# Attention scores over row halves in one stretch, and float32r passes for half of block 0

## The chip, the cores and the metric

The kernel runs on one core of a Trainium2 chip. The metric is the device time of one execution in microseconds; three executions of the kernel before gave 608.41, 609.69 and 610.22 us, a median of 609.69. The engines are PE (TensorE; PEld is its weight load), DVE (VectorE), ACT (ScalarE), POOL (GpSimd) and SP, whose queue issues the loads and stores.

## The reference

Attention with a window of 128 keys and 4 sink keys (2 batches, 8 heads, 768 positions, head size 64) feeds a network of 512 to 2048 to 512 with a leaky maximum, and that feeds a router with 8 experts.

```python
keep = is_sink | ((rel >= 0) & (rel < window))
a = softmax(where(keep, q @ k.T / sqrt(64), -1e9))       # per head
x = (a @ v)                                              # 1536 tokens x 512
h = x @ w_in; x = maximum(0.01 * h, h) @ w_out           # w_in 512x2048, w_out 2048x512
e = argmax(x @ w_gate)                                   # 8 experts, 384 places each
out = gate * (relu(x[place] @ w1[e]) @ w2[e])            # w1 512x1024, w2 1024x512
```

Results are held to float32 precision. The weights of the first network and of the experts come as float64.

## The kernel before, in words

The 1536 tokens are 12 tiles of 128 (six per batch), taken in 6 blocks of two tiles. For each block j, `build` walks the 16 column tiles f of the hidden layer: `first` makes 128 hidden columns for the block's 256 tokens in PSUM, `leak` applies the leaky maximum, `split_g` splits the result into a high and a low float32r part, and `second`, two column tiles later, multiplies with w_out and adds into two PSUM banks. A float32 product is kept exact in three float32r passes (high x high, high x low, low x high); block 0 instead takes one float32 pass, since its weights have only just come in.

Block 0 also turns the weights from float64 to float32 on DVE (`convert`, three DVE instructions for each half of a column tile), as they land from HBM. `split` makes the high (ACT) and low (POOL in block 0, DVE later) parts that the later blocks use.

Attention is cut into steps. One or two are put between `first` and `second` of a column tile, so that attention of tiles 2j+2 and 2j+3 runs inside block j. Tiles 0 and 1 ("plain") are done before block 0. A unit is four heads g of one tile t; it is worked off in two pairs pr, two steps apart. `pipeline` gives each function its step:

- `high_k`, `low_k`, `high_q`, `low_q`: high and low parts of k and q side by side, on ACT and DVE or POOL;
- `trans_k`, `trans_q`: eight float32r transposes (twelve for tiles 2 and 3) put both parts of a head on 128 partitions, so that a score is two full-height matmuls: (high, low) and (low, high) of q against (high, low) of k;
- `scores` (L501): four matmuls for a pair, into two of the four PSUM buffers of the tag "att"; ACT copies one half (L506), DVE copies the other under a mask (L513), and takes the maximum (L514);
- `exps` (L219), `norm` (L226, L227 on DVE, then POOL), `trans` (transposes of p, then L543: DVE multiplies by the masks of this tile and the one before; for tiles 2 and 3 ACT copies and POOL masks);
- `pv` (L572): float32 products with v, whose two heads of a pair go to the lower and upper 64 output partitions, that is to two column halves of the array.

The order on PE, ACT, POOL and SP is that of the program; on DVE a scheduler chooses it when the kernel is built. The four PSUM buffers "att" serve all of attention's steps and the router's transposes. In block 0 `first` has one PSUM buffer, later two.

Of the kernel before, what the change touches and what calls it, by code (L numbers as in the profile page):

```python
# [29 lines left out]
HQ = 3  # L30
SINK = 2
# [9 lines left out]
CLEAR_AT, CLEAR = 8, 2  # L41
ROUTE = (2, 5, 9, 10, 11, 14)
# [351 lines left out]
class RingAttention(Attention):  # L394
# [16 lines left out]
    def setup(self):  # L411
# [6 lines left out]
        self.kT = [c.tile([P, self.G, 2, self.W], F32R, name=f"kT{g}") for g in range(self.NG)]  # L418
# [45 lines left out]
        if SC:  # L464
            self.psk = [c.tile([P, 4, 32], F32, name=f"psk{n}") for n in range(2)]
            for t in self.psk:
                nc.gpsimd.memset(t, 0.0)
# [19 lines left out]
    def scores(self, t, g, pr):  # L487
        nc = self.nc
        b, i = divmod(t, self.NT)
        W = self.W  # L490
        pm = self.p["pp"].tile([P, 2, W], F32, tag="pm", name="pm")
        mx = self.p["sm"].tile([P, 2], F32, tag="mx", name="mx")
# [28 lines left out]
    def split_p(self, t, g, pr):  # L521

        pm, _, w = self.pu[t, g, pr]
        st = None
        if t % self.NT and self.SC:
            st = self.psk[pr % 2]
            self.nc.gpsimd.tensor_copy(st[:, 0:2, 0:self.SC], pm[:, :, P:])
        self.pu[t, g, pr] = (pm, st)

    def trans(self, t, g, pr):  # L530
        nc = self.nc
        i = t % self.NT
        pm, st = self.pu[t, g, pr]
        ps = self.p["ps"].tile([P, 3, P], F32, tag="att", name="pps")
        for e in range(2):
            nc.tensor.transpose(ps[:, e, :], pm[:, e, 0:P], self.ident)
        if st is not None:
            nc.tensor.transpose(ps[:, 2, :], st.rearrange("p a s -> p (a s)"), self.ident)  # L538
        n = 2 if i else 1
        pt = self.p["c"].tile([P, 2, 2, P], F32, tag="c", name="pt")[:, 0:n]  # L540
        src = ps[:, 0:2, :]
        if i and t >= EARLY:
            nc.vector.tensor_tensor(out=pt, in0=src.unsqueeze(1).to_broadcast([P, n, 2, P]),  # L543
# [1341 lines left out]
```

## Time and profile before

| | us |
|---|---|
| median of three executions | 609.69 |
| profiled execution, whole | 612.13 |
| its span in the trace | 610.3 |
| PE busy | 578.6 (95%) |
| PEld busy | 499.4 (82%) |
| DVE busy | 383.4 (63%) |
| ACT busy | 310.1 (51%) |
| POOL busy | 179.5 (29%) |

The span is what the trace covers; 1.8 us lie around it. Blocks 0 to 5 fill the span up to about 425 us, the router's end and the experts the rest. A matmul's recorded duration contains its way through the array and overlaps that of the next, so the cost of one in a full row of them is the distance from start to start. A float32 matmul stands in the trace as two records. "128*64" behind an instruction gives the rows and columns of the array that it uses.

### The profile page before, as it was taken

The page shows a single profiled execution, that of the slowest core. Times are in us where ns is not written, and L with a number is a line of the kernel's source. Part 1 is how long each engine was busy: PE and PEld are TensorE (multiplying, and loading weights), DVE is VectorE, ACT ScalarE, POOL GpSimd, SP SyncE. Part 2 cuts the span into 40 slices and gives each one's busy share as a digit, 9 for nine tenths or more (in the row PEclk, how much of TensorE's full clock was granted, in tenths as well). Part 3 has the DMA queues.
Part 4 walks back from the last instruction along what each step waited for, and adds up shares of the span by engine and source line. Part 5 has one row for each costly group of instructions (what it writes and reads, how often), then busy time and mean ns, then how long its engine had stood idle before and what let it go on. Part 6 is the DMA issues. An engine that isn't in the chain of part 4 may idle for free. (4 is left out here: it accounts for less than half of the span.)

```text
span 610.3 us, 11622 instructions
## 1 busy us (share of the span) xinstructions
PE 578.6 (95%) x3889; PEld 499.4 (82%) x3889; DVE 383.4 (63%) x908; ACT 310.1 (51%) x900; POOL 179.5 (29%) x328
## 2 busy tenths in 40 slices
PE   7688888999999999999999999999989999999994
PEld 7575656679989989999999988998788989998783
DVE  4798998368854565556655552276476766655992
ACT  4665555566655455545555433254253634434771
POOL 4425545542343234332432233123110120101110
PEclk9899999899999999999999999999989999999998
DMA  8769989521464402230223025755166766543950
GB/s 235 198 208 247 294 224 295 150 88 52 178 208 134 122 18 70 88 104 20 57 53 109 1 58 169 249 188 164 62 207 201 236 195 202 183 138 110 310 186 13
DMA packets 83564, 91.88 MB, mean 151 GB/s; under 512 B 42964, under 2 KB 51156, under 8 KB 83473
## 3 DMA queue, kind: packets, MB, share of 16 engines
q1 hardware_dynamic: 81488, 85.68, 46.9%
q0 software_dynamic: 1984, 5.13, 2.3%
q8 instruction: 39, 0.64, 0.4%
q14 instruction: 53, 0.43, 0.2%
HBM read 72.01 MB, written 20.09 MB: 151 GB/s over the span
## 5 line engine op out<-in xcount | busy, mean ns | idle before, releaser
L894 PE MATMUL y<-wh,gp 128*128 128x512 f32 x320 | 114.2, 397 | 0.5 <-ACT gp L874 0.5
L876 POOL TENSOR_TENSOR gp<-g,gp 128x256 fp32r<-128x256 f32 x77 | 56.9, 738 | 193.1 <-ACT gp L874 148.6
L848 PE MATMUL hps<-xth,wh 128*128 128x256 f32 x320 | 92.8, 290 | 0.0
L848 PE MATMUL hps<-xtl,wh 128*128 128x256 f32 x320 | 90.2, 282 | 0.0
L848 PE MATMUL hps<-xth,wl 128*128 128x256 f32 x320 | 90.1, 281 | 0.0
L1177 DVE TENSOR_TENSOR cw<-craw,cw 128x512 fp32r<-128x512 f32 x128 | 83.4, 695 | 9.0 <-ACT cw L1175 7.7
L1175 ACT CAST cw<-craw 128x512 fp32r<-128x512 f32 x112 | 63.4, 621 | 23.7 <-PE py L1362 23.0
L894 PEld LDWEIGHTS y<-wh,gp 128*128 128x128 f32 x320 | 60.2, 188 | 11.4 <-ACT gp L874 1.0
L1362 PE MATMUL py<-cw,ht 128*128 128x512 f32 x264 | 63.9, 398 | 0.2 <-DVE ht L1350 0.2
L848 PEld LDWEIGHTS hps<-xth,wh 128*128 128x128 f32 x320 | 60.4, 189 | 3.2 <-issue 0.6
L848 PEld LDWEIGHTS hps<-xtl,wh 128*128 128x128 f32 x320 | 60.3, 189 | 3.1 <-issue 0.7
L894 PE MATMUL y<-wl,gp 128*128 128x512 f32 x160 | 62.7, 392 | 0.0
L864 ACT ACTIVATE g<-hps 128x256 f32<-128x256 f32 x80 | 30.5, 381 | 61.5 <-PE hps L848 60.9
L1313 PE MATMUL ph<-xt,cw 128*128 128x256 f32 (+2 forms) x444 | 59.7, 296 | 1.3 <-DVE xt L1301 1.1
L848 PEld LDWEIGHTS hps<-xth,wl 128*128 128x128 f32 x320 | 60.7, 190 | 0.0
L1313 PEld LDWEIGHTS ph<-xt,cw 128*128 128x128 f32 x444 | 58.2, 195 | 1.8 <-DVE xt L1301 1.3
L1362 PEld LDWEIGHTS py<-cw,ht 128*128 128x128 f32 x264 | 49.1, 189 | 11.5 <-DVE ht L1350 0.7
L865 DVE TENSOR_TENSOR g<-hps,g 128x256 f32<-128x256 f32 x80 | 33.4, 417 | 25.0 <-ACT g L864 24.8
L874 ACT CAST gp<-g 128x256 fp32r<-128x256 f32 x80 | 33.3, 416 | 30.9 <-DVE g L865 30.6
L219 ACT ACTIVATE pm<-pm,mx 128x132 f32<-128x132 f32 (+1 forms) x80 | 31.7, 398 | 32.0 <-DVE mx L514 31.9
L1371 POOL DMA_INDIRECT out<-ys,gt x11 | 11.4, 1033 | 112.6 <-DVE ys L1370 112.6
L543 DVE TENSOR_TENSOR pt<-pps,both 128x512 f32<-128x512 f32 x28 | 19.2, 688 | 31.7 <-PE pps L538 31.7
(211 smaller groups left out, 1118.4 us busy)
## 6 DMA issues: line engine op xcount, KB each, us to landing
craw<-in_moe_w SPq DMA_DIRECT2D x128, 256.0 KB, 3.7
rawi<-in_moe_w_in SPq DMA_DIRECT2D x16, 512.0 KB, 4.4
rawo<-in_moe_w_out SPq DMA_DIRECT2D x16, 512.0 KB, 4.8
places<-zero SPq DMA_DIRECT2D x24, 257.0 KB, 6.7
wh<-wscr SPq DMA_DIRECT2D x16, 256.0 KB, 2.8
wl<-wscr SPq DMA_DIRECT2D x16, 256.0 KB, 3.1
xg<-places SPq DMA_DIRECT2D x12, 257.0 KB, 3.4
natv<-in_v SPq DMA_DIRECT2D x12, 256.0 KB, 6.5
```

The costliest lines, as they stand in the source:

```text
L219: nc.scalar.activation(pm[:, e, 0:w], pm[:, e, 0:w], AF.Exp, bias=mx[:, e:e + 1], accum_out=su[:, e:e + 1])
L543: nc.vector.tensor_tensor(out=pt, in0=src.unsqueeze(1).to_broadcast([P, n, 2, P]), in1=self.both.unsqueeze(2).to_broadcast([P, n, 2, P]), ...
L848: nc.tensor.matmul(ps, lhsT=w, rhs=x, start=(n == 0), stop=(n == len(mm) - 1))
L864: nc.scalar.activation(g, ps, AF.Copy, scale=0.01)
L865: nc.vector.tensor_tensor(out=g, in0=ps, in1=g, op=ALU.max)
L874: nc.scalar.copy(gp[:, 0], g)
L876: eng.tensor_tensor(out=gp[:, 1], in0=g, in1=gp[:, 0].bitcast(F32), op=ALU.subtract)
L894: nc.tensor.matmul(y, lhsT=l, rhs=r, start=(start and n == 0), stop=(stop and n == len(mm) - 1))
L1175: nc.scalar.copy(h, t)
L1177: eng.tensor_tensor(out=l, in0=t, in1=h.bitcast(F32), op=ALU.subtract)
L1313: nc.tensor.matmul(self.ph[f][:, sl], lhsT=self.w[e, "a", h, k][w][:, f * P:(f + 1) * P], rhs=self.xt[:, a, k, sl], start=(m == 0), stop=( ...
L1362: nc.tensor.matmul(self.py[n], lhsT=x, rhs=w, start=(h == 0 and f == 0 and m == 0), stop=(h == self.NH - 1 and f == self.HF - 1 and m == 2))
```

## The change

Four things change.

1. A unit is worked off as a whole, four steps to the next (`GROUP`). `turn` takes the place of the six functions that prepared q and k: two float32 transposes of q and two of k, each with two heads of 64 on 128 partitions, then the high part on ACT and the low part on DVE, straight from PSUM. The low part of k has a tile of its own; `keep_k` also serves tiles 0 and 1.
2. `scores` takes a head in three passes (high x high, high x low, low x high) over the 64 partitions where it lies. The two heads of a pair alternate, into different PSUM buffers, and the unit's twelve matmuls follow one another. They take all four "att" buffers. The reduction and the normalisation act on four heads at once, the latter three steps behind.
3. `trans` masks p on DVE for every tile, with one instruction for each of the two tiles of keys.
4. In block 0, column tiles 8 to 15 are handled in three float32r passes as in later blocks (`in_parts`). Their weights are split two column tiles ahead, by ACT and POOL; `split_x0` splits block 0's tokens once. `leak` of these tiles has its maximum on DVE.

```diff
+GROUP, NORM_AT, TRANS_AT, PV_AT = 4, 3, 5, 7
...
+    def keep_k(self, t, g, ps):
+
+        nc, SC, i = self.nc, self.SC, t % self.NT
+        hi, lo = ([k[:, :, i % 2, 0:P]] + [k[:, :, r, P:] for r in range(2 if i == 0 and SC else 0)]
+                  for k in self.kT[g])
+        for n, (h, l) in enumerate(zip(hi, lo)):
+            if n == 2:
+                nc.gpsimd.tensor_copy(h, hi[1].bitcast(F32))
+                nc.gpsimd.tensor_copy(l, lo[1].bitcast(F32))
+            elif n or t >= self.plain - 1:
+                src = ps[:, :, 0:SC] if n else ps
+                nc.scalar.copy(h, src)
+                nc.vector.tensor_tensor(out=l, in0=src, in1=h.bitcast(F32), op=ALU.subtract)
+
+    def turn(self, t, g):
+
+        nc, NP = self.nc, self.G // 2
+        ps = self.p["ps"].tile([P, 2, NP, P], F32, tag="att", name="qps")
+        for a, nm in enumerate("qk"):
+            for pr in range(NP):
+                x = self.heads(t, g, nm)[:, 2 * pr:2 * pr + 2, :]
+                nc.tensor.transpose(ps[:, a, pr, :], x.rearrange("p a d -> p (a d)"), self.ident)
+        qT = self.p["c"].tile([P, 2, NP, P], F32R, tag="c", name="qT")
+        nc.scalar.activation(qT[:, 0], ps[:, 0], AF.Copy, scale=self.scale)
+        nc.vector.scalar_tensor_tensor(out=qT[:, 1], in0=ps[:, 0], scalar=self.scale, in1=qT[:, 0].bitcast(F32),
+                                       op0=ALU.mult, op1=ALU.subtract)
+        self.qT[t, g] = qT
+        self.keep_k(t, g, ps[:, 1])
...
+    def scores(self, t, g):
+        nc, NP = self.nc, self.G // 2
+        i, W = t % self.NT, self.W
+        pm = self.p["pp"].tile([P, NP, 2, W], F32, tag="pm", name="pm")
+        mx = self.p["sm"].tile([P, NP, 2], F32, tag="mx", name="mx")
         own = i % 2
         w = W if i else P
-        sps = [self.p["ps"].tile([P, 2, W], F32, tag="att", name="sps") for e in range(2)]
-        for e in range(2):
-            h = 2 * pr + e
-            rhs = self.kT[g][:, h, :, :] if i else self.kT[g][:, h, 0, 0:P]
-            out = sps[e] if i else sps[e][:, 0, 0:P]
-            for vv in range(2):
-                nc.tensor.matmul(out, lhsT=self.qT[t, g][vv][:, h, :], rhs=rhs, start=(vv == 0), stop=(vv == 1))
-        for e in range(2):
-            if i == 0:
-                nc.vector.tensor_tensor(out=pm[:, e, 0:P], in0=sps[e][:, 0, 0:P], in1=self.m0, op=ALU.add)
-            else:
-                nc.scalar.copy(pm[:, e, :], sps[e][:, 1 - own, :])
+        sps = [[self.p["ps"].tile([P, 2, W], F32, tag="att", name="sps") for e in range(2)] for pr in range(NP)]
+        for pr in range(NP):
+            for n, (a, c) in enumerate(((0, 0), (0, 1), (1, 0))):
+                for e in range(2):
+                    r = slice(64 * e, 64 * e + 64)
+                    k = self.kT[g][c][r, pr]
+                    nc.tensor.matmul(sps[pr][e] if i else sps[pr][e][:, 0, 0:P], lhsT=self.qT[t, g][r, a, pr, :],
+                                     rhs=k if i else k[:, 0, 0:P], start=(n == 0), stop=(n == 2))
+        for pr in range(NP):
+            for e in range(2):
+                if i == 0:
+                    nc.vector.tensor_tensor(out=pm[:, pr, e, 0:P], in0=sps[pr][e][:, 0, 0:P], in1=self.m0, op=ALU.add)
+                else:
+                    nc.scalar.copy(pm[:, pr, e, :], sps[pr][e][:, 1 - own, :])
+                    nc.vector.copy_predicated(pm[:, pr, e, 0:P], self.sel.bitcast(I32), sps[pr][e][:, own, 0:P])
         if i == 1 and self.SC or i > 1 and self.n_sink < self.SC:
             m = self.m1 if i == 1 else self.m2
-            nc.vector.tensor_tensor(out=pm[:, :, P:], in0=pm[:, :, P:],
-                                    in1=m.unsqueeze(1).to_broadcast([P, 2, self.SC]), op=ALU.add)
-        if i:
-            for e in range(2):
-                nc.vector.copy_predicated(pm[:, e, 0:P], self.sel.bitcast(I32), sps[e][:, own, 0:P])
-        nc.vector.reduce_max(mx, pm[:, :, 0:w], axis=AX.X, negate=True)
-        self.pu[t, g, pr] = (pm, mx, w)
+            sk = pm[:, :, :, P:].rearrange("p a e c -> p (a e) c")
+            nc.vector.tensor_tensor(out=sk, in0=sk, in1=m.unsqueeze(1).to_broadcast([P, self.G, self.SC]), op=ALU.add)
+        nc.vector.reduce_max(mx.rearrange("p a e -> p (a e)"),
+                             pm[:, :, :, 0:w].rearrange("p a e c -> p (a e) c"), axis=AX.X, negate=True)
+        su = self.p["sm"].tile([P, NP, 2], F32, tag="su", name="su")
+        self.pu[t, g] = (pm, mx, su, w)
...
+        ps = self.p["ps"].tile([P, G, P], F32, tag="att", name="pps")
+        for h in range(G):
+            nc.tensor.transpose(ps[:, h, :], pm[:, h // 2, h % 2, 0:P], self.ident)
         sp = None
         if st is not None:
-            sp = self.p["pp"].tile([P, P], F32, tag="sp", name="sp")
-            nc.scalar.copy(sp, ps[:, 2, :])
-        self.pu[t, g, pr] = (pt, sp)
-
-    def pv(self, t, g, pr):
+            ps2 = self.p["ps"].tile([P, NP, P], F32, tag="att", name="kps2")
+            for pr in range(NP):
...
+        for x in range(2 if i else 1):
+            pt = self.p["c"].tile([P, G, P], F32, tag="c", name="pt")
+            if i:
+                nc.vector.tensor_tensor(out=pt, in0=ps, in1=self.both[:, x].unsqueeze(1).to_broadcast([P, G, P]),
+                                        op=ALU.mult)
+            else:
+                nc.scalar.copy(pt, ps)
+            pts.append(pt)
...
+        for t, g, s in units:
+            for pr in range(self.G // 2):
+                put(pre, s + 1 + pr, self.exps, t, g, pr)
...
+        for t, g, s in units:
+            put(mid, s, self.scores, t, g)
+            put(mid, s + TRANS_AT, self.trans, t, g)
+            put(mid, s + PV_AT, self.pv, t, g)
+            if g == self.NG - 1:
+                done[s + PV_AT] = t
+        for t, g, s in units:
+            if s:
+                put(mid, s - 1, self.turn, t, g)
...
+    def split_x0(self):
+
+        nc, c = self.nc, self.p["c"]
+        for k in range(0, self.K, 2):
+            x = self.xt(0)[0][:, k:k + 2, :]
+            h, l = (c.tile([P, 2, self.N], F32R, tag="c", name=nm) for nm in ("x0h", "x0l"))
+            nc.scalar.copy(h, x)
+            nc.gpsimd.tensor_tensor(out=l, in0=x, in1=h.bitcast(F32), op=ALU.subtract)
+            self.x0.append((h, l))
+
+    def in_parts(self, j, f):
+        return j > 0 or f in self.ahead
...
-        if j:
+        if self.in_parts(j, f):
             wh, wl = map(kc, self.w[f][0])
-            xh, xl = self.xt(j)
+            xh, xl = [[x[:, k, :] for k in range(self.K)] for x in self.xt(j)] if j else \
+                [[self.x0[k // 2][a][:, k % 2, :] for k in range(self.K)] for a in range(2)]
             mm = ((wh, xh), (wh, xl), (wl, xh))
         else:
-            mm = ((kc(self.v[f][0]), self.xt(j)[0]),)
-        mm = [(w[:, k, :], x[:, k, :]) for k in range(self.K) for w, x in mm]
+            x = self.xt(j)[0]
+            mm = ((kc(self.v[f][0]), [x[:, k, :] for k in range(self.K)]),)
+        mm = [(w[:, k, :], x[k]) for k in range(self.K) for w, x in mm]
...
-        if j == 0:
+        if not self.in_parts(j, f):
...
-                splits.extend((f, x) for x in range(2))
+                splits.extend((f, x) for x in range(0 if f in ffn.ahead else 2))
...
-                split(SPLIT[min(j, 1)])
+                if j == 0 and ring and i == AHEAD - 3:
+                    ffn.split_x0()
+                if j == 0 and ring and AHEAD <= i + 2 < ffn.NF:
+                    ffn.ahead.add(i + 2)
+                    for x in range(2):
+                        ffn.split(i + 2, x, nc.gpsimd)
+                else:
+                    split(SPLIT[min(j, 1)])
```

On PE, at the place in block 1 where a unit's product with v (ops) is followed by the preparation of the next unit (kps, qps: transposes of k and q), stood:

```order
L572 MATMUL ops<-pt,natv 64x128 x4
L572 MATMUL ops<-sp,vsraw 64x128 x2
L572 MATMUL ops<-pt,natv 64x128 x4
L572 MATMUL ops<-sp,vsraw 64x128 x2
L163 MATMUL kps<-ident_r,ks 128x128 x4
L197 MATMUL qps<-ident_r,qs 128x128 x4
```

and now stands:

```order
L613 MATMUL ops<-pt,natv 64x128 x4
L613 MATMUL ops<-sp,vsraw 64x128 x2
L613 MATMUL ops<-pt,natv 64x128 x4
L613 MATMUL ops<-sp,vsraw 64x128 x2
L504 MATMUL qps<-ident,natq 128x128 x2
L504 MATMUL qps<-ident,natk 128x128 x2
```

Eight float32r transposes have become four in float32.

At the scores (sps) of a unit in block 1, on PE, with the second product (y) behind them, before:

```order
L536 MATMUL pps<-ident,pm 128x128 x2
L538 MATMUL pps<-ident,psk_196 128x128
L501 MATMUL sps<-kT_126,qT 128x264 x4
L894 MATMUL y_1672<-wh,gp 128x512
L894 MATMUL y_1672<-wl,gp 128x512
L894 MATMUL y_1672<-wh,gp 128x512
L894 MATMUL y_1673<-wh,gp 128x512
L894 MATMUL y_1673<-wl,gp 128x512
L894 MATMUL y_1673<-wh,gp 128x512
```

and now, where kTh and kTl are the high and low parts of k:

```order
L532 MATMUL sps<-kTh_125,qT 128x264 x2
L532 MATMUL sps<-kTl_126,qT 128x264 x2
L532 MATMUL sps<-kTh_125,qT 128x264 x4
L532 MATMUL sps<-kTl_126,qT 128x264 x2
L532 MATMUL sps<-kTh_125,qT 128x264 x2
L984 MATMUL y_1662<-wh,gp 128x512
L984 MATMUL y_1662<-wl,gp 128x512
L984 MATMUL y_1662<-wh,gp 128x512
L984 MATMUL y_1663<-wh,gp 128x512
L984 MATMUL y_1663<-wl,gp 128x512
L984 MATMUL y_1663<-wh,gp 128x512
```

Before, this place comes twice in a unit, with a pair's transposes of p (pps) ahead of the scores; now it comes once, with twelve half-height matmuls, and all transposes of p stand together in the next step.

On DVE, at the end of the conversions in block 0 (the last `cvt<-rawo,word`), before:

```order
L514 TENSOR_REDUCE mx<-pm 128x2
L226 TENSOR_SCALAR ri<-su 128x2
L227 RECIPROCAL ri<-ri 128x2
L584 TENSOR_TENSOR xtl<-ops,xth 128x2x128
L202 CAST qT<-qps 64x512 x2
L796 SCALAR_TENSOR_TENSOR cvt<-rawo,word 128x512
L513 COPY_PREDICATED pm<-sel,sps 128x128 x2
L514 TENSOR_REDUCE mx<-pm 128x2
```

and now:

```order
L561 TENSOR_SCALAR ri<-su 128x4
L871 SCALAR_TENSOR_TENSOR cvt<-rawi,word 128x512
L955 TENSOR_TENSOR g<-hps,g 128x256
L562 RECIPROCAL ri<-ri 128x4
L861 TENSOR_SCALAR word<-rawo 128x512
L619 TENSOR_TENSOR xtl<-ops,xth 128x2x128
L507 SCALAR_TENSOR_TENSOR qT<-qps,qT 128x256
L865 SCALAR_TENSOR_TENSOR word<-rawo,word 128x512
L495 TENSOR_TENSOR kTl_126<-qps,kTh_125 128x2x128
L871 SCALAR_TENSOR_TENSOR cvt<-rawo,word 128x512
L955 TENSOR_TENSOR g<-hps,g 128x256
L540 COPY_PREDICATED pm<-sel,sps 128x128 x4
```

The last conversion stands between the preparation of tile 4's first unit and the masked copy of its scores in both; ri (L561, L562) has moved away from the reduction that it belongs to, with conversions between, and the maximum of `leak` (g) has come in.

## Rows read from the trace of the kernel before

**Rows 1.** Busy time by stretch: length, engines' busy (instructions), clock, DMA share, GB/s.

```profile
36.00:106.00 70.00, 60.44 (x334) 42.41 (x332) 62.42 (x122) 38.99 (x128) 34.33 (x53) 1.00 0.90 263
106.00:124.00 18.00, 17.80 (x86) 11.91 (x87) 7.15 (x17) 9.64 (x31) 10.81 (x17) 0.91 0.49 137
124.00:372.00 248.00, 247.91 (x1922) 223.97 (x1922) 146.82 (x419) 132.77 (x448) 83.34 (x139) 1.00 0.29 85
```

**Rows 2.** Waits of PE, 20 to 124 us: total us, times, longest.

```profile
PE qps L197 <- DVE pm L513: 5.6, 4, 2.5
...
PE sps L501 <- ACT qT L199: 1.1, 2, 0.7
PE sps L501 <- DVE qT L202: 1.0, 1, 1.0
```

**Rows 3.** Timeline of PE near 300 us: start, length, instruction, merged count.

```profile
301.64 0.28 PE L848 MATMUL hps<-xth,wh 128*128 128x256 f32 x1
...
303.06 0.39 PE L894 MATMUL y<-wh,gp 128*128 128x512 f32 x1
...
304.44 0.28 PE L848 MATMUL hps<-xth,wh 128*128 128x256 f32 x1
...
308.14 0.66 PE L572 MATMUL ops<-pt,natv 128*64 128x128 f32 x8
...
309.61 0.53 PE L163 MATMUL kps<-ident_r,ks 128*128 128x128 f32 x4
...
310.32 0.35 PE L848 MATMUL hps<-xth,wh 128*128 128x256 f32 x1
```

**Rows 4.** Timeline of PE: sixteen loads with short matmuls; four float32 transposes.

```profile
147.04 1.85 PE L979 MATMUL lps<-wg,x2T 128*128 128x8 f32 x16
148.74 0.37 PE L848 MATMUL hps<-xth,wh 128*128 128x256 f32 x1
...
433.90 0.60 PE L1347 MATMUL ph<-ident,hs 128*128 128x128 f32 x4
434.25 0.71 PE L1333 MATMUL ph<-cw,xt 128*128 128x512 f32 x2
```

**Rows 5.** Waits of PE's weight loads, whole run.

```profile
PEld kps L163 <- PE ops L572: 1.4, 8, 0.2
```

**Rows 6.** Timeline of PE in block 0, float32 products.

```profile
91.20 1.89 PE L848 MATMUL hps<-xth,cvt 128*128 128x256 f32 x8
92.92 1.88 PE L894 MATMUL y<-cvt,gr 128*128 128x512 f32 x4
94.64 1.89 PE L848 MATMUL hps<-xth,cvt 128*128 128x256 f32 x8
```

**Rows 7.** DVE groups, 36 to 107 us: busy, mean ns | idle before.

```profile
L226 DVE TENSOR_SCALAR ri<-su 128x2 f32<-128x2 f32 x8 | 4.0, 498 | 4.1 <-ACT pm L219 4.1
...
L202 DVE CAST qT<-qps 64x512 fp32r<-64x512 f32 x2 | 1.4, 688 | 0.5 <-ACT qT L199 0.5
```

**Rows 8.** Groups of instructions, whole run.

```profile
L865 DVE TENSOR_TENSOR g<-hps,g 128x256 f32<-128x256 f32 x80 | 33.4, 417 | 25.0 <-ACT g L864 24.8
...
L543 DVE TENSOR_TENSOR pt<-pps,both 128x512 f32<-128x512 f32 x28 | 19.2, 688 | 31.7 <-PE pps L538 31.7
...
L513 DVE COPY_PREDICATED pm<-sel,sps 128x128 f32<-128x128 int32 x72 | 18.3, 300 | 13.6 <-ACT pm L506 13.5
...
L506 ACT COPY pm<-sps 128x132 f32<-128x132 f32 x72 | 16.5, 291 | 0.2 <-POOL wl L817 0.2
```

**Rows 9.** Busy time by stretch, as Rows 1.

```profile
106.60:109.60 3.00, 3.00 (x6) 1.28 (x6) 2.76 (x7) 2.37 (x9) 3.00 (x5) 0.58 1.10 251
```

**Rows 10.** Timeline of PE after the last conversion.

```profile
106.67 3.20 PE L894 MATMUL y<-cvt,gr 128*128 128x512 f32 x4
109.67 2.31 PE L848 MATMUL hps<-xth,cvt 128*128 128x256 f32 x8
111.81 1.88 PE L894 MATMUL y<-cvt,gr 128*128 128x512 f32 x4
```

More of the change, by code (lines that the diff above doesn't have):

```diff
@@ L417, in setup @@
         self.W = P + SC
-        self.kT = [c.tile([P, self.G, 2, self.W], F32R, name=f"kT{g}") for g in range(self.NG)]
+        self.kT = [[c.tile([P, self.G // 2, 2, self.W], F32R, name=f"kT{a}{g}") for a in "hl"]
+                   for g in range(self.NG)]
         fill = NEG
@@ L464, in setup @@
         if SC:
-            self.psk = [c.tile([P, 4, 32], F32, name=f"psk{n}") for n in range(2)]
+            self.psk = [c.tile([P, self.G // 2, 4, 32], F32, name=f"psk{n}") for n in range(2)]
             for t in self.psk:
@@ new lines, in exps, with norm @@
+    def exps(self, t, g, pr):
+        pm, mx, su, w = self.pu[t, g]
+        for e in range(2):
+            a = pm[:, pr, e, 0:w]
+            self.nc.scalar.activation(a, a, AF.Exp, bias=mx[:, pr, e:e + 1], accum_out=su[:, pr, e:e + 1])
+    def norm(self, t, g):
+        nc, G, SC = self.nc, self.G, self.SC
+        pm, _, su, w = self.pu[t, g]
+        ri = self.p["sm"].tile([P, G], F32, tag="ri", name="ri")
+        nc.vector.tensor_scalar(out=ri, in0=su.rearrange("p a e -> p (a e)"), scalar1=1.0e-9, scalar2=None, op0=ALU.add)
+        nc.vector.reciprocal(ri, ri)
+        a = pm[:, :, :, 0:w].rearrange("p a e c -> p (a e) c")
+        nc.gpsimd.tensor_tensor(out=a, in0=a, in1=ri.unsqueeze(2).to_broadcast([P, G, w]), op=ALU.mult)
+        st = None
+        if t % self.NT and SC:
+            st = self.psk[g % 2]
+            nc.gpsimd.tensor_copy(st[:, :, 0:2, 0:SC], pm[:, :, :, P:])
+        self.pu[t, g] = (pm, st)
@@ L519, in prep_v @@
             self.load(t + 1, "v")
[L521 to L531, printed above, removed]
-        i = t % self.NT
[L533 to L543, printed above, removed]
-                                    in1=self.both.unsqueeze(2).to_broadcast([P, n, 2, P]), op=ALU.mult)
-        else:
-            nc.scalar.copy(pt, src.unsqueeze(1).to_broadcast([P, n, 2, P]))
-        for x in range(n if i and t < EARLY else 0):
-            sg = 1 - 2 * x
-            nc.gpsimd.affine_select(out=pt[:, x], in_=pt[:, x], pattern=[[0, 2], [sg, P]], compare_op=ALU.is_ge,
-                                    fill=0.0, base=-x, channel_multiplier=-sg)
@@ L576, in pv, with pipeline, put @@
         nc.scalar.copy(hi, ps)
[L577 to L584 removed]
+        if lo:
+            nc.vector.tensor_tensor(out=lo[0], in0=ps, in1=hi.bitcast(F32), op=ALU.subtract)
+    def pipeline(self, ts, n_first, first):
+        units, s = [], n_first
+        for t in ts:
+            for g in range(self.NG):
+                units.append((t, g, s))
+                s += GROUP
+        n_steps = s - GROUP + PV_AT + 1
+        pre, mid = ([[] for _ in range(n_steps)] for _ in range(2))
+        done = [None] * n_steps
+        def put(where, s, f, *a):
+            where[max(s, 0)].append(lambda: f(*a))
+        for s, after, f, *a in first:
+            if f is None:
+                done[s] = a[0]
+            else:
+                put(mid if after else pre, s, f, *a)
+        for t, g, s in units:
+            for pr in range(self.G // 2):
+                put(pre, s + 1 + pr, self.exps, t, g, pr)
+            put(pre, s + NORM_AT, self.norm, t, g)
+            if g == self.NG - 1:
+                put(pre, s - 2, self.load, t + 1, self.WITH_Q)
+            put(pre, s + 2, self.prep_v, t, g)
+            if not s:
+                put(pre, 0, self.turn, t, g)
+            if g == 0:
+                put(pre, s, self.tile_start, t)
+        for t, g, s in units:
+            put(mid, s, self.scores, t, g)
+            put(mid, s + TRANS_AT, self.trans, t, g)
+            put(mid, s + PV_AT, self.pv, t, g)
+            if g == self.NG - 1:
+                done[s + PV_AT] = t
+        for t, g, s in units:
+            if s:
+                put(mid, s - 1, self.turn, t, g)
+        return list(zip(done, pre, mid))
     def pv_tiles(self, t):
@@ L870, in split_g @@
         g = self.g[j, f]
-        if j == 0:
+        if not self.in_parts(j, f):
             return
```

51 lines of the change are left out of this document (24 added, 27 removed).

## The prediction

> **What bounds the kernel now.** I read the busy time by stretch first, then what PE waits for, then the start times of single PE instructions, then DVE's groups in the stretch where PE waits. In [rows 1] the reader is to see three regimes. From 124 to 372 us (blocks 1 to 4 of the first network, with the attention of tiles 4 to 11 woven in) PE is busy 247.9 of 248 us at a granted clock of 1.00, its upper level of 2.4 GHz, while DVE, ACT and POOL are busy 147, 133 and 83 us. A PE instruction that goes there shortens the run by what it took; work moved between the other engines costs nothing as long as PE is not made to wait. From 36 to 106 us (block 0) PE is busy 60.4 of 70 us and DVE 62.4: here DVE, which turns the float64 words of the weights into float32, sets the pace, and PE's longest waits are for DVE's masked score copy and for the casts of qT [rows 2]. From 106 to 124 us PE is full again, at a mean clock of 0.91. What comes after 425 us (router and experts) is not touched; I carry it over unchanged.
>
> A matmul's recorded duration overlaps its neighbour's, so I price PE by start to start. Twelve 256-column matmuls take 303.06 - 301.64 = 1.42 us, 0.118 each; six of 512 columns take 304.44 - 303.06 = 1.38 us, 0.230 each [rows 3]. Scores have 264 columns: 0.121 each.
>
> **The change, part by part.**
>
> *Transposes of q and k.* A unit (four heads of one tile) had eight float32r transposes from tile 4 on: 310.32 - 309.61 = 0.71 us [rows 3]. It now has four in float32, and four such elsewhere take 434.25 - 433.90 = 0.35 us [rows 4]. That is -0.36 us a unit. The ACT and DVE work around them shrinks as well, and off the path.
>
> *Scores.* Eight full-height matmuls (0.97 us) become twelve of half height, which alternate between partitions 0-63 and 64-127. If the two halves run at once, six slots of 0.121 make 0.73 us (-0.24). If they run one after the other, 1.45 us (+0.48). No row shows a half-height matmul. The nearest is the product with v, which fills column halves: 24 records start within 309.61 - 308.14 = 1.47 us [rows 3], 0.061 each. A 256-column record of the same float32 kind takes 1.72/8 = 0.215 us in block 0 [rows 6], so one of 128 columns alone is 0.107, and 24 are 2.58 us: halves there run 1.75 times as fast. By that ratio the twelve take 1.45/1.75 = 0.83 us, which I take: -0.14 us a unit.
>
> Between the ends lies the weight load. Sixteen loads of 128 columns, each followed by a matmul of only 8 columns, take 148.74 - 147.04 = 1.70 us, 0.106 each [rows 4]: that is what loads alone cost when they queue. Twelve would be 1.27 us (+0.30). In v's product a load has 64 columns, so that row cannot show whether loads of two halves queue. The Trainium skill, "TensorE: Matmul & The Clock Gate", section "LDWEIGHTS (loading the stationary operand)", says that a load's time goes with its columns and not its rows, so that halving the height saves nothing in a load; by this rule alone the scores would cost 0.30 us more. "TensorEngine Tiling (Array Packing)" of the Trainium skill, section "Key Properties", says that tiles load and multiply independently of each other; by it the loads pair up too, and the scores cost 0.24 us less.
>
> *Switching the array.* After v's product the loads of the next transposes stood idle for PE eight times, 1.4 us together, 0.175 each [rows 5], because they were not pulled ahead. Scores now enter and leave a half-array mode: two more switches. The 1.47 us above already hold one; I add 0.1 for the other. Bounds 0 and 0.35 for both.
>
> A unit comes to -0.36 - 0.14 + 0.10 = -0.40 us; 16 units (tiles 4 to 11, two each) give **-6.4 us**. The bounds of a unit are -0.60 (halves at once, no switch) and +0.32 (one after the other, 0.2 for switches).
>
> *New waits in that stretch.* The scores take all four PSUM buffers, so the transposes of p one step later wait for the first two to be emptied, and behind them on PE queue the second product and the next column tile. Between the two PE has one second product and one first, 1.38 + 1.42 = 2.8 us; ACT's four copies and DVE's four masked copies (0.29 and 0.30 us, [rows 8]) overlap to about 1.5 us. Likewise the scores wait for the low part of k on DVE, one ACT cast and two DVE steps of 0.42 us behind the transposes, with 2.8 us between. I take no wait. If the cover went, each unit would lose about 0.5 us, the whole gain.
>
> *Block 0, up to the last conversion.* DVE gains masks on p, two of 0.69 us, three units by then: 4.1 us; the low part of k, five of 0.42 (taken like L865), and the max of the leak, four of 0.42: 3.8 [rows 8]; one low part of q more, 0.4. It loses L202 (1.4) and half of L226 (2.0) [rows 7]. The reduction keeps its elements. That is +4.9 us. But L226 also stood still for 4.1 us, four times, for the exponentials of the reduction (L514) that stands directly ahead of it in DVE's order; in the new order conversions stand between the two, and with that wait gone the sum is +0.8. I take +1, bounds -1 and +5. PE's shorter work before that point is hidden by DVE. In both orders the last conversion stands between the q/k step of tile 4's first unit and its scores, so PE is at the same place when it ends.
>
> *Block 0, after it.* Column tiles 8 to 15 go from one float32 pass to three of float32r. A first product was 92.92 - 91.20 = 1.72 us and becomes 1.42; a second was 94.64 - 92.92 = 1.72 and becomes 1.38 [rows 6]. Behind the last conversion lie six seconds (10 to 15) and three firsts (13 to 15): -2.04 - 0.90 = -2.9 us. In the same place the granted clock was 0.58 [rows 9] after PE's waits of 0.7 and 1.0 us for qT [rows 2]: 109.67 - 106.67 = 3.00 us for a second product and 2.14 for the first behind it [rows 10], 1.7 us too much. The new order still has a wait for q and k there, so I count half of it as gone, -0.85. POOL now makes both low halves of a column tile in one step, two ahead of use; it is busy 34 of 70 us before [rows 1], so I give that no price in the middle and up to +2 at the end. Block 0: +1 - 2.9 - 0.85 = **-2.8 us**.
>
> *Before block 0* twelve transposes fall away (12 x 0.089 = 1.1 us) and two pairs of copies are added (at most 1.6 us, as 0.42 each on ACT and DVE); DVE paces what follows. I take 0.
>
> Sum: -6.4 - 2.8 = -9.2 us. The profiled execution took 612.1 us (span 610.3, 1.8 around it) and would take 602.9. It lies 2.4 us above the median of 609.69; taken off that, the forecast is **600.5 us**.
>
> **The rivals.**
>
> *The loads queue.* Halves multiply at once, but each of twelve loads takes 0.106 us: a unit is +0.30 - 0.36 + 0.20 = +0.14, 16 give +2.2, with block 0 at -2.8: 609.1 us, no change. For it: loads at 0.106 in [rows 4]. Against: v's product shows two halves of the array at work together.
>
> *The halves do not overlap at all* (the change then does not do what its name says), and this is the slower end: PE, in every scores step, 1.45 us for 0.97. A unit is +0.32, 16 give +5.1, block 0 -2.8: 612.0 us. It decides from twelve matmuls taking more than about 1.42 us, since then 16 units exceed block 0's gain by over 1.8 us. For it: no half-height row exists. Against: the same 1.75.
>
> *Block 0 gives nothing.* With one PSUM buffer for the first product there, PE's next column tile waits until DVE has done the max, which stands behind conversions; DVE ends 5 us later and eats the -2.9, for +2 to +3. With the units at -6.4: 606 us. For it: DVE 89% busy there. Against: L226's 4.1 us of standing.
>
> *More than I count.* Halves at once and no switch (-9.6), DVE 1 us earlier, the clock held (-5.6 in block 0): 594.5 us.
>
> **How the numbers follow.** Forecast 0.47 (its own range 596 to 605), loads queue 0.16, no overlap 0.14, block 0 gives nothing 0.12, more 0.11. A difference of 0.3%, 1.8 us, is about what a measurement of this kernel tells from no change. Faster: 0.47 + 0.12 + 0.11 = 0.70. Same: the queueing loads, 0.16. Slower: 0.14. The range reaches from the best case, 594.5, to the slow rival, 612; what lies outside is the worse half of the slow rival (block 0 late as well, 617) and a few in 100 below.
>
> **What the profile after would show.** The twelve score matmuls of a unit starting within 0.7 to 0.9 us (1.3: loads queue; 1.45: no overlap). q/k transposes at 0.35 us. PE full from block 1 to 4, and that stretch about 6 us shorter. The last conversion within 2 us of its old time, and block 1 begun about 3 us earlier. No wait of PE for the copies of the scores. I would be wrong if PE waited after the scores for DVE, or if block 0 ended later than before.

## The result, and the profile after

The changed kernel takes 603.1 us (median of 6 runs, 600.5 to 605.1) where the kernel before takes 609.96 (median of 6). The medians lie 6.9 us apart; the ratio on record is 0.986 (95%: 0.983 to 0.990), which of 609.96 is 8.5 us. The forecast was 600.5 with a range of 596 to 605, so the time came out as predicted. The terms of its sum did not. The profiled execution's span is 601.7 us against 610.3, and this table cuts three executions (one of the kernel before, two of the changed one) at the same places of the program. Starts are those of PE's first product of a block in the timeline; blocks 2 to 4 run from the first product of block 2 to that of block 5.

| us | before | changed | changed, second execution | forecast |
|---|---|---|---|---|
| first product of block 0 | 36.77 | 35.99 | 38.04 | same |
| from there to the end of the last conversion | 70.10 | 66.59 | 67.98 | +1 |
| from there to the first product of block 1 | 16.30 | 12.93 | 12.92 | about -3.1 |
| block 1 | 64.91 | 63.07 | 63.08 | -2.3 |
| blocks 2 to 4 | 186.49 | 185.08 | 185.08 | -4.8 |
| the rest (block 5, router, experts) | 235.7 | 238.0 | 233.3 | same |

(The prediction's -2.9 for block 0's products includes two seconds that run inside block 1, 0.7 us. Its -6.4 is spread here over four blocks.) The stretch before the last conversion gained where a loss was forecast, blocks 2 to 4 gained 1.41 us in place of 4.8, and the rest, the same instructions, scatters by 4.7 us from one execution to another.

The stretches of [rows 1] in the changed kernel:

```profile
36.00:106.00 70.00, 58.92 (x357) 42.38 (x356) 65.92 (x130) 35.34 (x119) 37.59 (x40) 0.98 0.84 251
106.00:124.00 18.00, 18.00 (x139) 15.82 (x138) 8.87 (x21) 12.29 (x36) 11.93 (x15) 1.00 0.96 286
124.00:372.00 248.00, 248.00 (x1941) 221.43 (x1941) 109.37 (x332) 114.10 (x387) 76.77 (x113) 1.00 0.30 86
```

PE is full from block 1 on, so none of the new waits appeared there. From 106 us on the granted clock is 1.00 where it was 0.91. Instead of [rows 2], PE's waits between 36 and 124 us are now:

```profile
PE hps L938 <- DVE g L955: 5.5, 4, 2.9
PE sps L532 <- ACT kTh L494: 3.1, 3, 2.7
PE hps L938 <- ACT gr L950: 2.0, 1, 2.0
```

The first row is the wait that a rival of the prediction described (block 0 gives nothing): a three-pass column tile's first product leaves its single PSUM buffer only when DVE has done the max, which stands behind conversions.

One stretch of twelve scores in a full block, PE's timeline (start, length, instruction, merged count):

```profile
240.67 0.28 PE L938 MATMUL hps<-xth,wl 128*128 128x256 f32 x1
240.88 0.39 PE L532 MATMUL sps<-kTh,qT 64*128 64x264 f32 x2
241.11 0.28 PE L532 MATMUL sps<-kTl,qT 64*128 64x264 f32 x2
241.23 0.41 PE L532 MATMUL sps<-kTh,qT 64*128 64x264 f32 x4
241.49 0.28 PE L532 MATMUL sps<-kTl,qT 64*128 64x264 f32 x2
241.60 0.28 PE L532 MATMUL sps<-kTh,qT 64*128 64x264 f32 x2
241.81 0.50 PE L984 MATMUL y<-wh,gp 128*128 128x512 f32 x1
242.16 0.40 PE L984 MATMUL y<-wl,gp 128*128 128x512 f32 x1
242.40 0.40 PE L984 MATMUL y<-wh,gp 128*128 128x512 f32 x1
```

The "x2" are pairs, one matmul of each half, that start together, in the middle of the stretch 0.12 us after the pair before: the halves run at once, and loads don't queue (twelve of 0.106 would be 1.27 us; the stretch takes 0.93). But the edges cost. From the last 256-column product to the first pair pass 240.88 - 240.67 = 0.21 us where 0.12 is usual, to the second pair 0.23 for 0.12, from the last pair to the second product 0.21 for 0.12, and to that product's next matmul 0.35 for [rows 3]'s 0.23.

Before the change, three transposes of p and the four scores of a pair stood together:

```profile
305.87 0.38 PE L536 MATMUL pps<-ident,pm 128*128 128x128 f32 x2
306.08 0.27 PE L538 MATMUL pps<-ident,psk 128*128 128x128 f32 x1
306.11 0.74 PE L501 MATMUL sps<-kT,qT 128*128 128x264 f32 x4
306.69 0.39 PE L894 MATMUL y<-wh,gp 128*128 128x512 f32 x1
```

The three take 0.24 to 0.25 us, the four 0.57 to 0.58, which is 0.09 more than four of 0.121.

The transposes of p, which now stand alone, and those of q and k:

```profile
292.77 0.60 PE L581 MATMUL pps<-ident,pm 128*128 128x128 f32 x4
293.21 0.38 PE L586 MATMUL kps<-ident,psk 128*128 128x128 f32 x2
293.35 0.47 PE L984 MATMUL y<-wh,gp 128*128 128x512 f32 x1
...
299.16 0.44 PE L504 MATMUL qps<-ident,natq 128*128 128x128 f32 x2
299.44 0.38 PE L504 MATMUL qps<-ident,natk 128*128 128x128 f32 x2
299.58 0.36 PE L938 MATMUL hps<-xth,wh 128*128 128x256 f32 x1
```

The latter take 0.42 us where [rows 3] had 0.71.

The stretch from the first product to the last conversion, of before:

```profile
36.77:106.87 70.10, 60.34 (x329) 42.30 (x328) 62.49 (x122) 38.94 (x129) 35.20 (x54) 1.00 0.91 262
```

and changed:

```profile
35.99:102.58 66.59, 55.51 (x334) 39.37 (x334) 63.99 (x124) 32.19 (x107) 34.17 (x37) 0.97 0.88 260
```

DVE (third number with a count) works 62.49 and 63.99 us there, 1.5 more; it stands idle for 7.6 us before and 2.6 after (64.26 and 3.7 in the second execution). Some of its groups from 50 us to the last conversion in the changed kernel:

```profile
L591 DVE TENSOR_TENSOR pt<-pps,both 128x512 f32<-128x512 f32 x6 | 3.8, 682 | 0.0
...
L955 DVE TENSOR_TENSOR g<-hps,g 128x256 f32<-128x256 f32 x4 | 1.6, 412 | 0.0
...
L561 DVE TENSOR_SCALAR ri<-su 128x4 f32<-128x4 f32 x3 | 0.5, 160 | 0.0
```

The last row answers to L226 of [rows 7]: 160 ns without a stand, where that mean was 498 ns beside 4.1 us of recorded idle time. Of L226's eight records in that stretch two take 1.22 us each and those that follow recorded idle time 0.17: its busy time held waiting as well.

### The profile page after: what moved, and what is told of

Read it like the earlier page. It is cut to its first block, busy times and chain, and to the rows that moved or that the text cites. A ratio compares the mean times of both kernels' runs of the same rounds, so it can differ in the third digit from the quotient of the medians.

```text
span 601.7 us, 11443 instructions
## 1 busy us (share of the span) xinstructions
PE 566.1 (94%) x3905; PEld 490.7 (82%) x3905; DVE 349.3 (58%) x832; ACT 285.4 (47%) x822; POOL 173.4 (29%) x284
## 5 line engine op out<-in xcount | busy, mean ns | idle before, releaser
L984 PE MATMUL y<-wh,gp 128*128 128x512 f32 x352 | 128.3, 405 | 0.4 <-ACT gp L964 0.4
L966 POOL TENSOR_TENSOR gp<-g,gp 128x256 fp32r<-128x256 f32 x85 | 62.8, 738 | 202.3 <-ACT gp L964 195.9
L955 DVE TENSOR_TENSOR g<-hps,g 128x256 f32<-128x256 f32 x88 | 37.0, 421 | 96.2 <-ACT g L954 95.6
L984 PEld LDWEIGHTS y<-wh,gp 128*128 128x128 f32 x352 | 66.1, 188 | 14.5 <-ACT gp L964 0.9
L984 PE MATMUL y<-wl,gp 128*128 128x512 f32 x176 | 68.8, 391 | 0.0
L954 ACT ACTIVATE g<-hps 128x256 f32<-128x256 f32 x88 | 33.6, 382 | 70.3 <-PE hps L938 69.9
L1452 PE MATMUL py<-cw,ht 128*128 128x512 f32 x264 | 63.9, 397 | 0.3 <-DVE ht L1440 0.3
L1403 PEld LDWEIGHTS ph<-xt,cw 128*128 128x128 f32 x444 | 59.6, 199 | 4.1 <-issue 2.7
L964 ACT CAST gp<-g 128x256 fp32r<-128x256 f32 x88 | 36.0, 409 | 43.9 <-DVE g L955 43.3
L984 PEld LDWEIGHTS y<-wl,gp 128*128 128x128 f32 x176 | 33.2, 189 | 3.8
```

What stands on the lines that cost most here:

```text
L954: nc.scalar.activation(g, ps, AF.Copy, scale=0.01)
L955: nc.vector.tensor_tensor(out=g, in0=ps, in1=g, op=ALU.max)
L964: nc.scalar.copy(gp[:, 0], g)
L966: eng.tensor_tensor(out=gp[:, 1], in0=g, in1=gp[:, 0].bitcast(F32), op=ALU.subtract)
L984: nc.tensor.matmul(y, lhsT=l, rhs=r, start=(start and n == 0), stop=(stop and n == len(mm) - 1))
L1403: nc.tensor.matmul(self.ph[f][:, sl], lhsT=self.w[e, "a", h, k][w][:, f * P:(f + 1) * P], rhs=self.xt[:, a, k, sl], start=(m == 0), stop=( ...
```

## Experiments

The runs were made on three occasions; each ratio is to the kernel before on the same chip and occasion. Ratios of different occasions are not compared closer than their intervals. Stages are read as in the table above.

### The attention part alone

```diff
-AHEAD = 8
+AHEAD = 99
```

> The changed kernel with block 0's last eight column tiles left in one float32 pass, as before the change: only the attention part of the change is in. Reading of the two traces: block 0 got 4.3 us shorter up to DVE's last conversion because DVE no longer stands for the exponentials, which is the attention part's doing; the three passes gave about 3 us behind the last conversion and cost DVE 1.3 us (four max of 0.33) ahead of it. Then this kernel takes 1.5 to 3 us more than the changed one, 604.5 to 606, its last conversion ends near 101.5 us, and block 0 (first to first product of block 1) lasts 81 to 82 us. Rival, the prediction's own split: the last conversion is at 107 to 108 us, block 0 lasts about 87 us, and blocks 1 to 4 are 6 us shorter than before the change. The time would be nearly the same, 604 to 605; the stages tell.

Measured: 604.2 us, ratio 0.988 (0.985 to 0.991), as the changed kernel. The stages decide for the first reading, and go further (block 0 was expected at 81 to 82 us and takes 78.4): first product to last conversion 64.5 us (before 70.1, changed 66.6 and 68.0), then 13.9 us to block 1 (16.3 and 12.9), block 1 64.1. So the attention part brought all of block 0's gain up to the last conversion, and most of that behind it, the clock among it. The three passes save 1.0 us behind the last conversion and 1.0 in block 1, and lose 2.1 to 3.5 ahead of it.

### DVE's stand taken out of the kernel before

```diff
-        nc.vector.tensor_scalar(out=ri, in0=su, scalar1=1.0e-9, scalar2=None, op0=ALU.add)
-        nc.vector.reciprocal(ri, ri)
+        if t < EARLY + 1:
+            nc.gpsimd.tensor_tensor(out=ri, in0=su, in1=self.minus, op=ALU.pow)
+        else:
+            nc.vector.tensor_scalar(out=ri, in0=su, scalar1=1.0e-9, scalar2=None, op0=ALU.add)
+            nc.vector.reciprocal(ri, ri)
...
```

> The kernel before the change with one edit: up to tile 4 the reciprocal of the sum of exponentials is made on POOL (one power instead of DVE's add and reciprocal), so that DVE never waits for the exponentials in block 0. Theory: DVE's standing at that place paced block 0. Its two small instructions and the standing before them held DVE for 7.3 us between 49.9 us and the last conversion, so the last conversion comes 6 to 7 us earlier, near 100 us, and the kernel takes 603 to 604.5. Rival: the standing was covered, and another wait (weights on POOL, casts on ACT, PE) takes its place: less than 2 us, 608 to 610.

Measured: 608.6 us, ratio 0.995 (0.992 to 0.997). First product to last conversion 66.7 us, 3.4 less. Half of what was expected came. DVE's busy time there is 3.3 us less than before and its standing about the same (7.5 us for 7.6). Its waits between 37 and 104 us say what took the reciprocal's place:

```profile
DVE xtl L589 <- ACT xth L581: 3.8, 3, 1.3
DVE pm L518 <- ACT pm L511: 1.4, 2, 0.8
```

The low part of v's product (L589), whose ACT cast comes late, stands in for the reciprocal. In the changed kernel's order conversions lie ahead of both, the reciprocal does not stand, and the low part stands 0.2 us (1.0 in the second execution). So a stand of DVE did pace block 0; to take away one of the two is worth half of what was expected.

### Halves not alternating

```diff
-        for pr in range(NP):
-            for n, (a, c) in enumerate(((0, 0), (0, 1), (1, 0))):
-                for e in range(2):
+        for e in range(2):
+            for pr in range(NP):
+                for n, (a, c) in enumerate(((0, 0), (0, 1), (1, 0))):
...
```

> The changed kernel with another order of the twelve score matmuls: first the six of partitions 0 to 63, then the six of 64 to 127, so that neighbours in the queue are of the same half. Theory: the halves run at once only where they alternate. Then twelve take 12 x 0.121 = 1.45 us instead of 0.93: +0.5 a unit, 16 units in full blocks: +8 us, 611 to 612. Rival, the halves did not overlap in the first place and the 0.93 us have another reason (a half-height matmul is simply faster): no change, 603.

Measured: 610.8 us, ratio 0.999 (0.996 to 1.002); blocks 2 to 4 188.89 us, 3.8 more, 0.32 a unit where 0.5 was expected; that the time is close to the expected 611 to 612 is in part luck. The order matters, but the halves still overlap in part:

```profile
246.18 0.39 PE L532 MATMUL sps<-kTh,qT 64*128 64x264 f32 x1
246.41 0.28 PE L532 MATMUL sps<-kTl,qT 64*128 64x264 f32 x1
246.53 0.41 PE L532 MATMUL sps<-kTh,qT 64*128 64x264 f32 x3
246.77 0.29 PE L532 MATMUL sps<-kTl,qT 64*128 64x264 f32 x2
246.89 0.40 PE L532 MATMUL sps<-kTh,qT 64*128 64x264 f32 x3
247.13 0.28 PE L532 MATMUL sps<-kTl,qT 64*128 64x264 f32 x1
247.25 0.28 PE L532 MATMUL sps<-kTh,qT 64*128 64x264 f32 x1
247.46 0.50 PE L984 MATMUL y<-wh,gp 128*128 128x512 f32 x1
```

Two single ones, then pairs from 246.53 on, then single ones again, 1.28 us in all. Six of one half were queued first; the seventh, of the other half, starts with the third. The names show it: in queue order the fifth record would be one of kTl, and it is one of kTh. The rival (the halves never overlapped, so that their order is without effect) is out.

### Scores in two stretches

```diff
-GROUP, NORM_AT, TRANS_AT, PV_AT = 4, 3, 5, 7
+GROUP, NORM_AT, TRANS_AT, PV_AT = 4, 4, 5, 7
...
-            put(mid, s, self.scores, t, g)
+            for pr in range(self.G // 2):
+                put(mid, s + 2 * pr, self.scores, t, g, pr)
```

Each `scores` then makes six matmuls.

> The changed kernel with the scores of a unit in two stretches of six, two steps apart (and the maximum for each pair of heads, the sum's reciprocal a step later). Theory: entering the half-height mode costs 0.09 us and leaving it 0.12, beyond the matmuls. Then a unit is 0.21 us longer, 12 units of blocks 2 to 4 make +2.5 us, 16 make +3.4. In block 0 DVE's order has the sum's reciprocal directly behind the second maximum again, so that it stands some 1 us for the exponentials in two or three places: +1 to +3 us there. Together 606.5 to 609.5. Rival: entering and leaving are free, the twelve matmuls take what they take: blocks 2 to 4 unchanged, and only block 0's part shows, 603 to 606.

Measured: 618.0 us, ratio 1.009 (1.006 to 1.013), more than expected. Blocks 2 to 4 are 4.6 us longer, 0.38 a unit, where 0.21 was expected, and no wait of PE is recorded in them; the stretch up to the last conversion is 69.5 us. One of the two stretches:

```profile
251.46 0.28 PE L937 MATMUL hps<-xth,wl 128*128 128x256 f32 x1
251.68 0.39 PE L534 MATMUL sps<-kTh,qT 64*128 64x264 f32 x2
251.90 0.29 PE L534 MATMUL sps<-kTl,qT 64*128 64x264 f32 x2
252.03 0.28 PE L534 MATMUL sps<-kTh,qT 64*128 64x264 f32 x2
252.24 0.49 PE L983 MATMUL y<-wh,gp 128*128 128x512 f32 x1
```

Six take 252.24 - 251.68 = 0.56 us, twelve 0.93: six more cost 0.37, 0.062 each, which is half of 0.121. Past the edges the halves overlap fully. What is left is a fixed price for each stretch, about 0.4 us (0.38 a unit for the second one), that I had put at 0.2.

### Masks and leak off DVE

```diff
-            if i:
+            if i and t < EARLY:
+                nc.scalar.copy(pt, ps)
...
-        if not self.in_parts(j, f):
+        if j == 0:
```

The first part takes the masks off DVE (a copy on ACT, then a select on POOL), the second the max of `leak` (two instructions on ACT, then POOL); each alone and both together were run.

> The changed kernel with the causal masks on p of tiles 2 and 3 made by a copy on ACT and a select on POOL, as before the change, in place of DVE's two products (0.60 us each from start to start, six of them up to the last conversion). Theory: after the change DVE works through block 0 nearly without standing (1.6 us in 52.7), so what is taken off it comes off the stage: last conversion 3 to 3.6 us earlier, 599.5 to 600.5 where the changed kernel is 603. Rival: another engine's chain (POOL, with six selects of some 0.8 us twice, or PE) is next in line, and less than 1.5 us comes of it, 602 to 603.

> The changed kernel with block 0's leak of the three-pass column tiles made by two ACT instructions and a POOL subtract, as in the other column tiles, in place of DVE's max. PE's waits of 5.5 us for that max go. Theory: those waits lie beside DVE's conversions, which set the pace, so that only the four max of 0.33 us themselves count: last conversion 1.3 us earlier, 601.5 to 602.5. Rival, the one of the prediction by which the single PSUM buffer of the first product makes block 0 late: with the 5.5 us of waits gone, block 0 ends 4 to 5 us earlier, 598 to 599.

> The masks and the leak of block 0 both off DVE. Theory (DVE paces block 0): the two add up, last conversion 4.3 to 4.9 us earlier than in the changed kernel, 598 to 599. Rival: POOL, which then has 12 more selects and 8 more subtracts, or PE takes over as the bound, and no more comes than from the masks alone.

Measured: ratios 0.992 (0.987 to 0.996) for the masks, 0.993 (0.990 to 0.997) for the leak, 0.991 (0.988 to 0.995) for both; none is shown to be faster than the changed kernel. The last conversion does come earlier after the first product, 64.4, 64.9 and 63.9 us against 66.6 and 68.0, but 14.7, 14.6 and 15.2 us follow it instead of 12.9, and block 0 lasts 79.1, 79.6 and 79.2 us against 79.5 and 80.9. With the masks gone from DVE, PE waits 3.0 us for DVE's max until 94.7 us, and its clock (last number but two) falls to the lower level, 1.2 GHz:

```profile
90.00:95.00 5.00, 2.04 (x11) 1.42 (x10) 4.69 (x8) 2.69 (x9) 2.95 (x4) 0.90 1.09 265
95.00:100.00 5.00, 5.00 (x18) 4.10 (x18) 4.10 (x10) 2.32 (x8) 3.22 (x3) 0.50 1.05 310
```

With both gone that wait is replaced by one for the high part of k:

```profile
PE sps L532 <- ACT kTh L494: 7.1, 3, 2.7
```

With the leak alone off DVE, too, other waits of PE grow where the 5.5 us for the max were:

```profile
PE sps L532 <- ACT kTh L494: 6.4, 3, 2.9
PE hps L938 <- ACT gr L950: 3.3, 3, 2.0
```

So taking work off DVE shortens block 0 by 1.8 us at most (79.1 against 80.9) before waits for ACT take over. My theory that the gains add up is wrong. The rival by which block 0 would end 4 to 5 us earlier without the waits for the max is wrong too: without them it is as long.

### Transposes of q and k behind those of p

```diff
-                put(mid, s - 1, self.turn, t, g)
+                put(mid, s - (3 if t >= EARLY else 1), self.turn, t, g)
```

> The changed kernel with the transposes of q and k from tile 4 on two steps earlier, directly behind the transposes of p of the unit two before, so that the six and the four make one stretch on PE. Theory: what keeps the units from being cheaper is a price of some 0.09 us at each change between float32 transposes and float32r products, so that one change less a unit gives 0.09 to 0.12 us: 12 units of blocks 2 to 4 are 1.1 to 1.5 us shorter together, the kernel 1.5 to 2 us, 601 to 601.5. Rival: the price belongs to the transposes themselves or moves to v's product, which then stands alone: blocks 2 to 4 unchanged, 603; if the earlier loads of q and k come late, longer.

Measured: 606.3 us, ratio 0.991 (0.987 to 0.995). Blocks 2 to 4 185.77 us, 0.7 more: the rival. The six and the four make one stretch, but the product with v, which now stands alone, pays the same price when the second product follows it (0.33 us between that product's first two matmuls, for 0.23):

```profile
257.48 0.39 PE L613 MATMUL ops<-sp,vsraw 128*64 128x128 f32 x4
257.80 0.50 PE L984 MATMUL y<-wh,gp 128*128 128x512 f32 x1
258.13 0.39 PE L984 MATMUL y<-wl,gp 128*128 128x512 f32 x1
```

In the traces of this case each float32 stretch that was read pays it before a float32r product. The other half of the rival came as well: block 1 is 1.6 us longer than in the changed kernel, since its earlier transposes wait for the load of q:

```profile
PE qps L504 <- DMA natq<-in_q: 1.3, 1, 1.3
```

### The changed kernel again, and idle matmuls against the clock

```diff
-            self.keep_warm(ps[0:64, 0, :], 4)
+            self.keep_warm(ps[0:64, 0, :], (4, 16)[g])
```

(in the last three; the third with AHEAD = 99, the fourth with AHEAD = 12)

> The changed kernel itself, once more, beside its variants. Two readings of its first trace are to be tested on a second one. First, PE's stand of 2.7 us in the experts with no releaser: every kernel with block 0's three passes profiled so far has one of 1.6 to 2.8 us at the same matmul, and neither the kernel before nor the one with the attention part alone has it there; so it stands here again, 1.5 to 2.9 us. Second, the granted clock of 1.00 from 28 to 36 us was luck: here it falls below 0.8 in that stretch, as in most others, and block 0 begins near 38 us rather than 36. Then the time is 603 to 606. Rival: both belong to single executions, the stand is gone or elsewhere, 600 to 602.

> The changed kernel with twelve more idle matmuls on the identity ahead of the second product with v, where PE otherwise waits 2.8 us for ACT. Theory: PE has no long wait there, the granted clock stays at 1.00 up to 36 us, block 0 begins near 36 us in every execution: 1.5 to 2.5 us less than the changed kernel in the same run, 601 to 602.5. They also shift PE's instructions behind them; if the stand in the experts hangs on where the program lies in memory or in its loads, it moves or goes (up to 2.7 us less). Rival: the idle matmuls are late themselves, and block 0 begins no earlier: 603 to 604.

> The attention part alone (all of block 0 in one float32 pass) with the same twelve idle matmuls. Theory: the three passes were worth nothing, since what they save behind the last conversion they lose in block 0's DVE work, in PE's waits and in the stand in the experts: this kernel is as fast as the changed one with the idle matmuls or up to 2 us faster, 600 to 602.5. Rival: the three passes are worth their 2.9 us, 603.5 to 605.5.

> The changed kernel with the idle matmuls and only the last four column tiles of block 0 in three passes instead of eight. Theory: only what lies behind the last conversion pays, so four column tiles give most of the 2.9 us and leave DVE the max of one of them only ahead of its last conversion: 0.5 to 2 us less than with eight, 599.5 to 601.5. Rival: what is saved behind the last conversion is lost to PE's waits and its clock in any case, no difference to the other two, 601 to 602.5.

Measured: the changed kernel 603.8 us, ratio 0.987 (0.983 to 0.992); with idle matmuls 603.9, 0.987 (0.982 to 0.992); the attention part alone with them 600.6, 0.982 (0.978 to 0.985); the last four column tiles in three passes with them 600.6, 0.982 (0.978 to 0.985). From 28 to 36 us, in the first and second execution of the changed kernel and with idle matmuls:

```profile
28.00:36.00 8.00, 6.45 (x61) 4.90 (x62) 6.03 (x10) 4.46 (x11) 1.16 (x3) 1.00 0.75 234
```

```profile
28.00:36.00 8.00, 5.76 (x40) 4.45 (x40) 6.77 (x13) 4.22 (x11) 1.63 (x3) 0.79 0.79 242
```

```profile
28.00:36.00 8.00, 7.20 (x69) 5.57 (x68) 6.77 (x13) 4.61 (x11) 1.63 (x3) 1.00 0.82 244
```

The clock there (last but two) does vary for one and the same kernel, and in the three profiles with idle matmuls it is 1.00 and block 0 begins at 36.7 to 36.8 us. That is about what was expected; the 1.5 to 2.5 us that it was to save are not seen in the changed kernel's time. The two fastest kernels measured lie 3.1 us below the changed one in the medians of one occasion, but the intervals overlap. On neither occasion does the attention part alone show a gain from the eight three-pass column tiles. From the first product of block 0 to that of block 5, three profiles with eight such tiles take 327.7, 329.1 and 327.8 us, two with none 327.6 each, the one with four 325.9. So eight are worth nothing there and may cost up to 1.4 us; that four save 1.7 rests on one profile. What else separates these kernels' profiles lies outside that stretch, most of it in the rest, where all kernels have the same instructions.

## Why the prediction was right, and where it was not

*Transposes of q and k*: right, 0.42 us for 0.71, of -0.36 forecast -0.29 came.

*Scores*: the mechanism was right and the size too careful. The six slots of 0.121 came true, -0.24 and not -0.14. This agrees with the Trainium skill, "TensorEngine Tiling (Array Packing)", section "Key Properties" (tiles load and multiply independently): six pairs start together, and twelve matmuls take 0.93 us. That a load's time goes with its columns (the Trainium skill, "TensorE: Matmul & The Clock Gate", section "LDWEIGHTS (loading the stationary operand)") does not mean that loads of two halves queue: that rival's 1.27 us did not come.

*Switching the array*: the term that was mis-sized. It stood at +0.10 with a bound of 0.35; the two-stretch kernel shows about 0.4 for each stretch of scores. Set against it is what scores paid before behind p's transposes: eight of 0.121 make 0.97, and four took 0.57, so 0.09 twice. And one piece was missing: p's six transposes, now alone, take 0.58 us and 0.09 at the change back to float32r, where before they took 0.50 beside scores. The sum held no term for them. A unit is -0.29 - 0.24 + 0.4 - 0.18 + 0.16 = -0.15 us; blocks 2 to 4 measure -1.41/12 = -0.12. So the units gave about 2 us of the 6.4.

*New waits in full blocks*: none, as forecast.

*Block 0 up to the last conversion*: this step failed, +1 forecast and -2.1 to -3.5 measured, outside its bounds. The term that was mis-sized is DVE's added work. It was taken as a sum of recorded durations, +4.9 us; by the time in which DVE is busy it is +1.5. Neighbours overlap (six masks take 0.60 each from start to start, the max 0.33), the reductions take 0.6 less, which was not counted, and L226 and L227 fell from eight each to four. At 0.16 for each of its eight records, some 2.7 of L226's 4.0 us were a stand, so removing half of them was too little. And DVE's standing fell by 5.0 us (3.9 in the second execution), where I had counted 4.1 and let the added work eat it. The kernel before without that stand and its two small instructions shows that they are worth 3.4 us even alone.

*Block 0 after the last conversion*: right in size by luck, -3.4 measured for -3.1. Without the three passes -2.4 of it is there too, as the clock does not fall there (1.00 from 105 to 110 us) and the work stands differently, where -0.85 was forecast; the passes add -1.0, where -2.2 was. With block 1's part they give 2.0 us, and take 2.1 to 3.5 ahead of the conversion. Block 0 as a whole, to the first product of block 1, is 5.5 to 6.9 us shorter, nearer to the rival "more than I count" (-5.6 there) than to the forecast.

*Before block 0 at nothing*: the term is nearer +1. The seven profiles whose kernels are the changed one up to there begin block 0 between 36.0 and 39.1 us, at 38.0 on average; the two with the order of before begin it at 36.8 and 37.0. *The experts at nothing*: the rest lies between 232.7 and 242.7 us in the fourteen profiles, with 1330 matmul records in each, so it scatters by more than any term of the sum.

So the forecast's total came from errors of opposite sign, by luck: units 4.2 us too good, block 0 (with its passes' part in block 1) 3.7 to 5.1 too bad.

## What to carry to other kernels

Price a busy in-order engine from start to start or by its busy time over a stretch, and look at a small instruction whose mean is three times its like: it holds a stand, and the order around it may be worth more than the work. Count mode changes of the array by stretches, each with a fixed price, and fill a stretch rather than open another. When a total comes true, check the terms at the same places of the program before you believe the account.

## What was not expected of the hardware

Matmuls of the two halves of the array can start out of queue order: with six of one half queued first (halves not alternating, above), the other half's first one started with the third, 246.53 us for both.

PE stood in the experts without a releaser in nine profiles of eight kernels, 1.1 to 2.8 us, as here in the changed one:

```profile
490.80 1.47 PE L1403 MATMUL ph<-xt,cw 128*128 128x128 f32 x10 [2.67 <-issue]
```

All nine have 3905 matmul records, and it stands at the 3342nd to 3348th of them, also where 24 idle ones at the start and 24 fewer in block 0 cancel. The five profiles with 3857, 3881, 3889 or 3929 records have none over 0.23 us. So in these profiles it goes with the length of PE's program and a place in it rather than with the passes as such; its cause stays open. In the second execution of the changed kernel it was 1.1 us, less than expected.
